# Moving the first MLP weight's products behind the last segment, with a reordered opening and refitted order tables

## The chip, the cores and the metric

One core of a Trainium2 chip. The time is device microseconds (us) of one execution; lower is better. A kernel counts as faster or slower from 2% on.

## The reference, cut to what matters

A recurrent attention over 64 segments of 32 tokens, with 8 memory tokens that come out of the segment before, and then an MLP over all 2048 tokens:

```python
for s in range(n_seg):                        # 64, one after the other: mem is carried
    h = concat([mem, x[s]])                   # 8 + 32 tokens, width 512
    q, k, v = h @ Wq, h @ Wk, h @ Wv          # 32 heads of 128
    p = softmax(where(mask, q @ k.T * scale, -1e9))
    o = (p @ v) @ Wo
    mem = o[:8]; outs.append(o[8:])
h = x + attention(layernorm(x))
out = h + gelu(layernorm(h) @ w1 + b1) @ w2 + b2      # F = 1792
```

Because of `mem` the segments can't overlap freely. What doesn't depend on the memory (the "B" products of a later block of four segments, here called filler work of the loop) is put between.

## The kernel before: the parts that matter

Segments are counted 0 to 63; four of them make a block of 128 tokens, so segments 4, 8, 12 ... are the first of a block. The kernel records operations and a list scheduler puts each on its engine by assumed times and by fitted priorities (`BONUS`). TensorE's order is given by a table, with a bank for each part:

```python
PHASE = (164, 250, 155, 235)
BONUS = {..., "nma": -1.85, ..., "xr": 5.47}                   # cut
ORDER = (("Q1", 0, 2), ("Q0", 0, 4), ("Q1", 2, 4), ("K0", 0, 4), ("K1", 0, 4), ("V0", 0, 4), ("SC0", 0, 99), ("F", 0, 1), ("SA", 0, 99), ("SC1", 0, 99),
         ("V1", 0, 4), ("F", 1, 2), ("PV0", 0, 99), ("F", 2, 3), ("PV1", 0, 99), ("WO", 0, 8), ("PVA", 0, 99), ("F", 3, 4))
```

Q, K and V are projections (L744, L490), SC0 and SC1 the two scores of the memory rows (L889), SA the scores of the other tokens (L947), PV0 and PV1 their products with the values (L919, L923), WO the output product (L1009), PVA the value product of the other tokens (L977), F the filler.

TensorE's instructions are fetched in pages of 256. `PHASE` says at which place of a page, modulo 256, each of the four kinds of segment shall begin; repeated weight loads serve as padding:

```python
if PHASE and o.tag is not None and o.tag[0] != seg:
    seg = o.tag[0]
    owed = (PHASE[seg % 4] - at) % FETCH_N        # FETCH_N = 256
    if owed > FETCH_N - SLIP:
        owed = 0
```

In the last block the filler place is taken by `w1_first`, four products of the first MLP weight and a Gelu on ScalarE:

```python
if bk == NTB - 1 and sg < 3:
    w1_first(2 * sg + r, BANK["F%d" % r])      # segments 60, 61, 62: six of the fourteen groups
```

## Time and profile before

858.89 us (three runs, 858.42 to 859.45). One profile:

| stretch | us | what |
|---|---|---|
| to 57.15 | 57.15 | opening: weights are loaded, segment 0 |
| 57.15 to 90.47 | 33.32 | segments 1 to 3, no filler |
| 90.47 to 695.22 | 604.75 | segments 4 to 59 ("the loop") |
| 695.22 to 749.61 | 54.39 | segments 60 to 63, up to the last output product |
| 749.61 to 780.61 | 31.00 | rest of the first MLP weight, MLP block 0 |
| 780.61 to the end | 76.29 | MLP blocks 1 to 3 |

The stretch table of the kernel before; columns are start:end, length, then busy time of PE, PEld, DVE, ACT and POOL with instruction counts, TensorE's granted clock, DMA share, GB/s. Rows that the prediction shows are left out:

```profile
57.15:90.47 33.32, 27.79 (x824) 18.63 (x1205) 25.98 (x82) 21.72 (x67) 11.50 (x30) 1.00 0.18 28
90.47:695.22 604.75, 601.04 (x17024) 346.43 (x18636) 495.19 (x1511) 439.55 (x1345) 196.19 (x525) 1.00 0.12 29
780.61:856.90 76.29, 72.91 (x330) 32.03 (x336) 16.35 (x24) 28.87 (x42) 17.66 (x16) 1.00 0.21 58
```

In the loop TensorE's records leave 604.75 - 601.04 = 3.7 us idle in 56 segments. (The ends of its products are modelled, so a short wait behind a product can hide in its record.)

### The profile page before, as it was taken

The page shows a single profiled execution, that of the slowest core. Times are in us where ns is not written, and L with a number is a line of the kernel's source. Part 1 is how long each engine was busy: PE and PEld are TensorE (multiplying, and loading weights), DVE is VectorE, ACT ScalarE, POOL GpSimd, SP SyncE. Part 2 cuts the span into 40 slices and gives each one's busy share as a digit, 9 for nine tenths or more (in the row PEclk, how much of TensorE's full clock was granted, in tenths as well). Part 3 has the DMA queues.
Part 4 walks back from the last instruction along what each step waited for, and adds up shares of the span by engine and source line. Part 5 has one row for each costly group of instructions (what it writes and reads, how often), then busy time and mean ns, then how long its engine had stood idle before and what let it go on. Part 6 is the DMA issues. An engine that isn't in the chain of part 4 may idle for free.

```text
span 856.9 us, 47407 instructions
## 1 busy us (share of the span) xinstructions
PE 804.1 (94%) x20064; PEld 448.2 (52%) x22282; DVE 597.3 (70%) x1782; ACT 561.7 (66%) x1609; POOL 263.5 (31%) x686
## 2 busy tenths in 40 slices
PE   3588999999999999999999999999999997799998
PEld 1245555556555555555555555555555553454443
DVE  3257777888787888788878787878787865533211
ACT  2346777777777777777777776777777778842332
POOL 3024114242424242333333324232414241047200
PEclk9879999999999999999999999999999999999999
DMA  9971000111101010101010101010122120154300
GB/s 345 352 196 22 10 17 23 29 29 29 29 25 32 24 34 24 33 23 35 22 35 20 36 21 33 19 26 17 28 47 52 47 78 16 39 177 120 86 25 24
DMA packets 66615, 48.80 MB, mean 57 GB/s; under 512 B 29156, under 2 KB 62828, under 8 KB 66412
## 3 DMA queue, kind: packets, MB, share of 16 engines
q1 hardware_dynamic: 66080, 45.50, 18.5%
q8 instruction: 166, 2.72, 1.4%
q14 instruction: 37, 0.30, 0.1%
q10 hardware_dynamic: 332, 0.27, 0.1%
HBM read 31.34 MB, written 8.39 MB: 46 GB/s over the span
## 4 chain that ended last, share of the span: by engine, by line
PE 84%; DVE 5%; ACT 5%; DMA 4%; issue 1%; SPq 0%; POOL 0%; ACTq 0%; DVEq 0%; POOLq 0%
PE ps L744 38%; PE ps L1009 13%; PE ps L490 8%; PE quad L1362 5%; PE ps L1355 4%; PE quad L919 3%; PE ps L1036 3%; PE quad L977 2%; PE quad L889 2%; ACT EC L901 2%; PE ps L947 2%; DMA WQ<-in_A_Wq_dram 1%; DVE TT L1021 1%; PE ps L1164 1%; DVE hT L1015 1%
## 5 line engine op out<-in xcount | busy, mean ns | idle before, releaser
L762 ACT CAST OT<-quad 128x128 bf16<-128x128 f32 (+1 forms) x192 | 85.0, 442 | 119.1 <-PE quad L977 78.8
L970 POOL COPY BD<-PTA 32x192 bf16<-32x192 bf16 x256 | 87.5, 342 | 228.7 <-DVE PTA L966 216.8
L744 PE MATMUL ps<-WQ,hT 128*32 128x512 bf16 x2048 | 124.8, 382 | 9.8 <-DVE hT L1015 8.0
L1009 PE MATMUL ps<-WO,OT 128*32 128x256 bf16 x4224 | 130.7, 275 | 1.5 <-ACT OT L762 1.5
L744 PE MATMUL ps<-WV,hT 128*32 128x512 bf16 x1780 | 121.4, 380 | 0.5 <-issue 0.5
L1009 PEld LDWEIGHTS ps<-WO,OT 128*32 128x32 bf16 x4224 | 107.4, 97 | 10.6 <-issue 2.6
L763 ACT ACTIVATE kq<-ps 128x512 bf16<-128x512 f32 x146 | 80.4, 596 | 48.2 <-PE ps L744 47.7
L744 PE MATMUL ps<-WK,hT 128*32 128x512 bf16 x1544 | 107.9, 380 | 0.0
L742 PEld LDWEIGHTS <-hT 128*32 128x32 bf16 x3652 | 60.3, 96 | 63.7 <-DVE hT L1015 38.0
L762 ACT CAST kq<-ps 128x512 bf16<-128x512 f32 x146 | 86.1, 591 | 11.2 <-PE ps L744 6.0
L785 DVE STREAM_TRANSPOSE KALL<-kq 128x256 f32<-128x256 f32 x160 | 68.9, 437 | 27.8 <-ACT kq L762 24.8
L762 ACT CAST VS<-ps 128x512 bf16<-128x512 f32 x124 | 72.4, 584 | 16.4 <-PE ps L744 14.1
L901 ACT ACTIVATE EC<-quad,nmc 128x64 f32<-128x64 f32 x252 | 76.8, 310 | 9.1 <-DVE nmc L897 3.6
L744 PEld LDWEIGHTS ps<-WV,hT 128*32 128x32 bf16 x1780 | 48.1, 96 | 42.1 <-issue 19.3
L744 PEld LDWEIGHTS ps<-WK,hT 128*32 128x32 bf16 x1544 | 46.4, 96 | 43.4 <-issue 23.2
L785 DVE STREAM_TRANSPOSE QT<-kq 128x256 f32<-128x256 f32 x128 | 55.7, 436 | 14.7 <-ACT kq L763 10.6
L919 PEld LDWEIGHTS quad<-PTC,VS 32*128 32x128 bf16 x2048 | 24.5, 92 | 75.9 <-ACT OT L762 29.1
L744 PEld LDWEIGHTS ps<-WQ,hT 128*32 128x32 bf16 x2048 | 55.0, 94 | 17.3 <-issue 1.7
L1358 ACT ACTIVATE WQ<-ps,b1t 128x512 bf16<-128x512 f32 x42 | 28.9, 687 | 52.8 <-PE ps L1355 52.8
L806 POOL COPY ZC<-QTB 128x256 bf16<-128x256 bf16 x64 | 25.3, 398 | 118.6 <-PE quad L889 81.9
L960 DVE TENSOR_REDUCE sma<-SA 128x8 f32<-128x256 f32 x64 | 26.8, 419 | 43.4 <-ACT SA L959 43.4
L490 PE MATMUL ps<-WK,hT 128*32 128x512 bf16 x504 | 51.5, 379 | 0.0
(155 smaller groups left out, 1516.6 us busy)
## 6 DMA issues: line engine op xcount, KB each, us to landing
WV<-in_A_Wv_dram SPq DMA_DIRECT2D x4, 1024.0 KB, 10.2
WK<-in_A_Wk_dram SPq DMA_DIRECT2D x4, 1024.0 KB, 19.2
v_last<-VSB SPq DMA_DIRECT2D x64, 64.0 KB, 2.5
WQ<-in_A_Wq_dram SPq DMA_DIRECT2D x4, 1024.0 KB, 10.2
VBD<-v_last SPq DMA_DIRECT2D x64, 64.0 KB, 2.5
WO<-in_A_Wo_dram SPq DMA_DIRECT2D x16, 256.0 KB, 7.5
h_mid<-xr SPq DMA_DIRECT2D x16, 128.0 KB, 2.0
WQ<-h_mid SPq DMA_DIRECT2D x4, 512.0 KB, 4.3
```

The lines of the kernel that those rows point to most:

```text
L490: return e.add_instruction(mybir.InstMatmult(name="I-%d" % (4000000 + _kept[0]), engine=mybir.EngineType.PE, start_tensor_calc=start, stop ...
L742: e.ldweights(l, tile_position=(0, 32 * j))
L744: ins = e.matmul(o, l, m, start=(k == 0), stop=(k == DC - 1), tile_position=(0, 32 * j), skip_group_check=True)
L762: return {"act": (lambda e: e.copy(out, src), t_act(n, ps_)), "dve": (lambda e: e.tensor_copy(out, src), 0.16 + 1.042e-3 * n * fast)}
L763: return {"act": (lambda e: e.mul(out, src, scale_), t_act(n, ps_)), "dve": (lambda e: e.tensor_scalar(out, src, scale_, None, ALU.mult), ...
L785: S.op("dve", lambda e: e.transpose(out, src), reads=[("kq", i)], writes=[key], dur=t_dve(256) + 0.02)
L901: ins = e.activation(EC[:, r, sl, :], o[:, sl, :], ACTF.Exp, bias=nmc[:, r, sl:sl + 1], accum_out=smc[:, r, sl:sl + 1])
L919: e.matmul(quad[:, j, (4 * r + i) * 16:(4 * r + i) * 16 + 16], VS[rows, s % 3, r, i * E:(i + 1) * E], PTC[rows, r, c0:c0 + 16, i // 2], st ...
L970: S.narrow(S.op("pool", lambda e, j=j, rows=rows: e.tensor_copy(BD[rows, par, :, j, :, :], PTA[rows, :, 0:NA, :]), reads=["PTA"], writes=[ ...
L1009: ins = e.matmul(ps[bank][32 * j:32 * j + 32, 0:256], lhs(slot(h)), wo_cols(h, b), start=(k == 0), stop=(k == 15), tile_position=(0, 32 * ...
L1355: ins = e.matmul(ps[bank][:, 0:SBT], W1[:, cc, fc * P:(fc + 1) * P], hnT_of(k)[:, cc, :], start=(cc == 0), stop=(cc == DC - 1))
L1362: S.op("pe", lambda e: e.matmul(quad[:, t, :], gT_of(k, fc)[:, t * P:(t + 1) * P], W2[:, fc, :], start=(fc == 0), stop=(fc == FC - 1)), re ...
```

## The change

Intent: take the Gelus, and with them the activation table loads, out of the last segments; bring the weights in before the value fetch of block 0; drop the filler in the opening; and fit TensorE's order, the banks, the priorities and the page phases anew.

```diff
-PHASE = (164, 250, 155, 235)
+PHASE = (109, 215, 114, 200)
-BONUS = {...}                                    # ~75 fitted priorities, all new; cut
+BONUS = {...}
-ORDER = (("Q1", 0, 2), ("Q0", 0, 4), ("Q1", 2, 4), ("K0", 0, 4), ("K1", 0, 4), ("V0", 0, 4), ("SC0", 0, 99), ("F", 0, 1), ("SA", 0, 99), ("SC1", 0, 99), ("V1",
-         0, 4), ("F", 1, 2), ("PV0", 0, 99), ("F", 2, 3), ("PV1", 0, 99), ("WO", 0, 8), ("PVA", 0, 99), ("F", 3, 4))
+ORDER = (("Q0", 0, 4), ("K0", 0, 4), ("Q1", 0, 4), ("K1", 0, 4), ("SC0", 0, 99), ("V0", 0, 4), ("V1", 0, 2), ("SC1", 0, 99), ("SA", 0, 99), ("V1", 2, 4), ("F",
+         0, 2), ("PV0", 0, 99), ("F", 2, 3), ("PV1", 0, 99), ("WO", 0, 8), ("PVA", 0, 99), ("F", 3, 4))
-         ("B", "Q", 1, (1, 6)), ("T", "WO", 3, 5), ("W", 7, 4), ("T", "WO", 5, 6), ("W", 7, 4), ("T", "WO", 6, 7), ("W", 7, 4), ("T", "WO", 7, 8))
+         ("B", "Q", 1, (1, 6)), ("T", "WO", 3, 8))
-                if bk == NTB - 1 and sg < 3:
-                    w1_first(2 * sg + r, BANK["F%d" % r])
-                chain[10:10] = spread["in", 0]
+                chain[14:14] = spread["in", 0]
-        for fc in range(6, FC):
-            w1_first(fc, (4, 5)[fc % 2])
-            rest[fc - 6]()
+        for fc in range(FC):
+            w1_first(fc, early[fc % 2])
+            rest.get(fc, lambda: None)()
```

(Cut: the new banks, the list of loads in the last segments, the new places of the remaining output products in `rest`, and two lines that follow from the move.)

## The prediction

> **What bounds the kernel now.** I read the stretch table first, cut where TensorE starts segments 1, 4, 56 and 60, the last output product of segment 63, the second MLP product and the second MLP block.
>
> ```profile
> core 0: us, PE busy (x) PEld busy (x) DVE busy (x) ACT busy (x) POOL busy (x), PEclk, DMA share, GB/s
> 90.47:652.00 561.53, 558.25 (x15808) 321.63 (x17302) 460.20 (x1405) 408.50 (x1250) 182.74 (x489) 1.00 0.11 28
> 695.22:749.61 54.39, 42.52 (x1066) 23.41 (x1313) 31.39 (x101) 45.62 (x101) 12.76 (x34) 0.97 0.13 37
> 749.61:767.86 18.25, 16.38 (x289) 9.38 (x282) 8.58 (x23) 8.44 (x13) 7.83 (x20) 1.00 0.53 159
> 767.86:780.61 12.75, 11.98 (x55) 5.32 (x55) 1.30 (x3) 0.69 (x1) 6.56 (x18) 1.00 0.58 153
> ```
>
> Segments 4 to 55 take 561.53 / 52 = 10.80 us each, TensorE nearly always busy. The last four take 54.39 us up to the last output product; there TensorE is busy only 42.5 and ScalarE 45.6. The chain of waits there, for segment 61:
>
> ```profile
> 709.48 1.92 PE ps L744 x32
> 714.63 1.28 ACT L901
> 719.15 1.28 ACT L1168
> 720.45 0.69 ACT hT L1168
> 721.71 1.28 ACT L959
> 724.94 1.92 PE ps L744 x32
> ```
>
> Segment 61 lasts 724.94 - 709.48 = 15.46 us, and three 1.28 us pieces of its chain are activation table loads: a Gelu (L1168) stands between two Exps (L901, L959). Next the opening: the chain, then stretches of 2 us.
>
> ```profile
> 20.39 7.36 DMA v_last<-VSB
> 30.11 10.95 DMA WQ<-in_A_Wq_dram
> 54.83 0.97 PE ps L713 x4
> 56.18 0.46 DVE TT L1021
> 57.15 1.92 PE ps L744 x32
> ```
> ```profile
> 30.00:32.00 2.00, 2.00 (x34) 0.86 (x25) 0.45 (x1) 0.80 (x2) 0.00 (x0) 0.71 1.01 182
> 36.00:38.00 2.00, 0.24 (x8) 0.00 (x0) 0.89 (x2) 1.27 (x4) 0.00 (x0) 1.00 1.03 409
> 48.00:50.00 2.00, 1.89 (x80) 1.71 (x84) 1.22 (x3) 1.16 (x5) 0.00 (x0) 0.50 1.11 349
> 54.00:56.00 2.00, 2.00 (x23) 0.55 (x20) 0.00 (x0) 0.00 (x0) 0.00 (x0) 1.00 0.37 105
> ```
>
> The value store of block 0 lands at about 27.8; its fetch waits for that in the queue, and half of WQ stands behind the fetch. The queue runs thin (182 GB/s), WQ lands at 41.1, and TensorE idles from 36 to 41. Then it runs at half clock until 51.6. By 54 DMA is falling off, the output weights are in, and TensorE does filler (L713) between output products.
>
> **What the Trainium skill says.** "ScalarE: Activation LUTs", section "What ACT_TABLE_LOAD costs": a load is about 1283 ns, with some 1380 ns of drain. The trace agrees on 1.28; no drain shows (714.63 + 1.28 = 715.91, the Exp starts at 715.93), so I count 1.28 alone. The same page, "Table sets: the hidden batching unit", says to finish all calls of one set before switching; the change does that. "TensorE: Matmul & The Clock Gate", section "What's actually happening": the array falls to half clock after an idle window of about 3.4 us and recovers after as much sustained work. Here: five thin microseconds, then 0.50. Its "Architectural detail" section calls the queues of ScalarE and VectorE strict FIFO; so an early instruction of theirs that waits holds all later ones.
>
> **The change, part by part.**
>
> *Segments 60 to 63.* The instruction listing of the built program has 14 table loads before and 2 after. What is segment 61 without loads and Gelus? Subtracting three loads, 15.46 - 3.85 = 11.6, and the Gelus it no longer carries (two of 0.69, partly on the path) bring 10.2 to 11.6. The second way is segment 3, which has neither filler nor Gelu: 79.86 to 90.47, 10.61 us. The third is the chain in the new order, from durations of an ordinary segment: Q0, K0, Q1, K1 end at 4 x 0.865 = 3.46; first score to its reduce 0.39; but the new VectorE order puts the second score's reduce and the wide one (L957) ahead of the first probabilities, so the second score at 4.9 gives reduce 5.29, wide one 5.58, PC 5.97, transpose 6.31, first PV 6.69 with 0.15 hop; PV1 0.79 later, output product 0.24 later, and 2.95 from there to the next Q (508.19 to 511.14): 10.67. I take 10.65. The output product of segment 63 starts 7.7 into it. So 3 x 10.65 + 7.7 = 39.7, against 54.39: **-14.5**, with 0.2 kept for slips.
>
> *Work moved behind.* Six of 14 groups of the first MLP weight (four 512-column products at 0.2155, 0.86 us) now come after segment 63: 6 x 0.86 = 5.2. In the listing, up to four groups follow each other with no other product between, on two banks; Gelu 0.69 plus a hop of 0.25 against 0.86 costs about 0.1 at each of some five such places: +0.5. Against that, the old code waited 1.68 us for VectorE's TTB (752.5 to 754.2, the bank of the last block product); the new code picks two other banks: -1.7. Smaller gaps of the old stage (18.25 - 16.38 less that) mostly close, -0.5, while the one remaining table load and the first Gelu are hidden by an output product between groups 0 and 1. 18.25 + 5.2 + 0.5 - 1.7 - 0.5 = 21.7: **+3.5**. The transposes for MLP block 1, 0.72 us late before, now stand ahead of the last three pieces of the first weight, and have 3 us more: **-0.7**.
>
> *The opening.* In the new queue all of WQ and two pieces of WO go before the value fetch. Up to 30 us 10.87 MB have moved (282, 401 and 404 GB/s over ten each); WV, WK, WQ, first inputs and the value store are 13.1 MB; at 0.40 MB/us the rest takes 5.6: WQ is there at 35.6, when TensorE first asks (36.1). Its products then end at about 37.9 instead of 43.5. After that WO sets the pace: 17.56 MB with the fetch, the last 4.4 at 0.35 MB/us: 48.3, and 12 filler products (2.6 us) are gone. Output product 0.35, then 1.4 to segment 1: near 50 at best against 57.15. But TensorE, waiting for WO piece by piece, may be cold, which would cost about 2 in segment 1. I take **-5**.
>
> *The 56 ordinary segments.* Start to start on TensorE (segment from 500.26): six projections 5.19, scores and SA 0.48, PV 0.68, WO 1.87, PVA 0.45, filler 1.72, sum 10.39; the best segments take 10.68 because of three waits: first PV for its probabilities (0.16), second PV for the copy of the first (0.12), Q for memory (0.2). The new order brings score 0 forward by 1.3 us, which takes away only the first. Minus 0.16 if nothing new comes. But with score 0 at 3.46, K0 and its query copy have to be transposed by then, and VectorE has opT 0.53, PA 0.44, mask 0.25, PTA 0.31 and two block transposes (0.38 each) ahead; adding spacings I get 3.5 to 3.8. And L957 ahead of the probabilities pushes first PV to 6.7, nearly where it is (464 - 457.25 = 6.71). So a computed 10.65 to 10.76, against a best of 10.68 and a mean of 10.80. The 0.12 between mean and best are hiccups, which the refitted phases may change either way. I take -0.05 each: **-2.8**, give or take 4.
>
> Sum: -14.5 + 3.5 - 0.7 - 5 - 2.8 = -19.5; 858.9 - 19.5 = **839.4 us**.
>
> **Rivals.** (a) *The refit loses in the loop.* If score 0 waits 0.3 us for VectorE in most segments, 56 x 0.2 = +11 over my term: about 853. For it: VectorE is busy 460 of 561 us and strictly in order; the block's mask, transposes and opT are ahead of K0. Against it: back-to-back transposes start 0.33 to 0.40 apart, less than their 0.45, and somebody refitted all priorities. (b) *The refit wins in the loop*, 0.15 a segment, hiccups included: -8 instead of -3, about 834. For it: 0.48 us of waits stand in each best segment. Against it: the wait for memory and the one between PVs are untouched. (c) *The opening gains little*, as WO is transfer-bound and TensorE stays cold without the filler: -2, total 842. The 0.50 clock for ten microseconds after only five thin ones speaks for it; that WQ no longer leaves that hole, against. (d) *The tail takes back more*: the normalisation of MLP block 1 (L1113, four of about 0.36) stands on VectorE before PTA of segment 63 and waits for its load; if that lands later than about 7 us after the output product, PVA of segment 63 and all Gelus behind its copy wait: +2 to 3.
>
> **Range and chances.** The table-load term is good to 1.5, tail 1.5, opening 2.5, loop 4; independent, that is about 5.2, so 80% is some 6.7 either side: 832.5 to 846.5. The 2% line lies near 841.9, just above the centre: faster 0.66, same 0.33, slower 0.01.
>
> **What will show it.** Table loads: two; segments 60 to 62 at 10.4 to 10.9 between first Q products. Output product of segment 63 to the second MLP product: 21 to 22.5. WQ landed before 37, no half clock at 42 to 46, segment 1 from 51 to 53. Mean of segments 4 to 55 at 10.68 to 10.82; if above 10.85 with TensorE waiting for KALL or ZC at the first score, rival (a) is right; below 10.68, rival (b). The prediction falls if the last segments stay over 11.5 (then the loads were not the cause), or if the loop moves by over 0.15 a segment.

## More of the kernel before

The residual addition of a finished block waits for a DMA transpose, and stands on VectorE, a strict queue, where the scheduler thinks the transpose will be done (its assumed time is worked out from the 256):

```python
def nat(bk):
    S.dma(lambda e: e.dma_start_transpose(oN[:], opT[:, bk % 2]...), 256, reads=[...], writes=["oN"])       # L1055, cut
    S.op("dve", lambda e: e.tensor_tensor(xs, xs, oN[:]..., ALU.add), reads=["oN", ("xr", bk % XR)], ...)   # L1058, cut
```

## The result, and the profile after

850.37 us (four runs, 849.34 to 852.85) against 858.96 us for the kernel before beside it. The ratio is 0.9904, 95% interval 0.9882 to 0.9927: within 2%, and 11 us above the predicted time, outside the predicted range of 832.5 to 846.5. All outputs are right. (Ratios are the mean time of one kernel's runs over that of the other's of the same rounds, so not quite the ratio of the medians.)

The stretch table of the changed kernel, cut at the same events. The profiled run is the slowest of the four (852.85 us), so the differences below sum to -5.9 us, those of the medians to -8.6:

```profile
54.16:89.36 35.20, 30.17 (x825) 21.46 (x1186) 24.95 (x82) 22.17 (x67) 11.39 (x30) 0.92 0.18 33
89.36:698.67 609.31, 601.79 (x17025) 334.69 (x18637) 467.21 (x1554) 443.05 (x1303) 195.78 (x526) 1.00 0.11 29
698.67:740.03 41.36, 36.05 (x1041) 22.11 (x1344) 29.55 (x95) 28.97 (x89) 12.65 (x34) 0.96 0.12 34
740.03:761.82 21.79, 21.78 (x313) 11.26 (x306) 8.54 (x22) 12.64 (x19) 12.18 (x32) 1.00 0.77 205
761.82:773.90 12.08, 12.08 (x57) 5.49 (x56) 3.28 (x6) 0.71 (x2) 6.58 (x10) 1.00 0.31 92
773.90:851.00 77.10, 73.23 (x337) 32.04 (x335) 14.38 (x22) 28.88 (x42) 13.46 (x12) 1.00 0.20 55
```

| stretch | before | after | difference | predicted |
|---|---|---|---|---|
| opening | 57.15 | 54.16 | -3.0 | -5, with segments 1 to 3 |
| segments 1 to 3 | 33.32 | 35.20 | +1.9 | |
| loop, segments 4 to 59 | 604.75 | 609.31 | +4.6 | -2.8 |
| segments 60 to 63 | 54.39 | 41.36 | -13.0 | -14.5 |
| to the second MLP product | 18.25 | 21.79 | +3.5 | +3.5 |
| MLP block 0 | 12.75 | 12.08 | -0.7 | -0.7 |
| rest | 76.29 | 77.10 | +0.8 | 0 |

The loop is where the sign was wrong. TensorE's busy time in it is the same within a microsecond (601.0 and 601.8); its idle time doubled, from 3.7 to 7.5 us. The idle time lies in two kinds of place. The first, in TensorE's timeline of segment 12 (start, length, engine, line, operands, count, idle before):

```profile
182.57 0.39 PE L490 MATMUL ps<-WK,hB 128*32 128x512 bf16 x4
182.90 0.23 PE L919 MATMUL quad<-PTC,VS 32*128 32x16 bf16 x9
183.99 0.21 PE L919 MATMUL quad<-PTC,VS 32*128 32x16 bf16 x7 [0.86 <-issue]
184.17 0.40 PE L1009 MATMUL ps<-WO,OT 128*32 128x256 bf16 x8
```

and of segment 28, the same products without the gap:

```profile
357.39 0.39 PE L490 MATMUL ps<-WK,hB 128*32 128x512 bf16 x4
357.72 0.40 PE L919 MATMUL quad<-PTC,VS 32*128 32x16 bf16 x16
357.96 0.21 PE L923 MATMUL quad<-PTC,VBD 32*128 32x64 bf16 x4
```

The second PV stops after its ninth product, for a reason that the profile can't name ("issue"). By the listing of the built program a page border lies there: instruction 18 of the 40 of PV1. The border before it is at the end of score 0 (31 of 32). The Trainium skill, "Runtime: NRT & Kernel Launch", section "Instruction fetch mechanics", says that instructions come in pages of 16 KiB (256 instructions), fetched by DMA while the page before runs, at a cost it calls "mostly hidden". The page size agrees: the instruction queue of TensorE moved 2.72 MB in 166 packets, 16 KB each. The DMA view of 178.9 to 184.4 us, segment 12 from the end of score 0 on; its first line is the rate in 40 slices of 0.1375 us:

```profile
GB/s 0 60 0 0 0 0 0 0 0 0 0 0 0 0 0 0 0 119 0 0 0 0 0 0 0 0 0 0 0 0 0 0 0 0 0 0 0 0 0 0
q8 instruction: 1, 0.02, 1.5%
```

The one packet of that queue (q8) starts in the 18th slice, 2.28 us after score 0, and lands 1.28 later; nothing else is on the DMA engines at that moment. PV1 goes on 1.5 us after the landing. In segment 28 the packet starts 0.93 after score 0, and nothing stops. This holds in all seven profiles with a border in that part of PV1 (segments 8, 12 ... 56, 91 in all; the runs are told below): in 33 the packet started 2.1 to 2.8 us after score 0, and all 33 stalled, by 0.21 to 0.89 us; in 58 it started 0.4 to 1.5 us after, and none of them lost more than 0.07 us there. In all 33, PV1 went on 1.2 to 1.6 us after the packet had landed; in the other 58 it had landed at least 1.7 us before the first product behind the border. (`old_prio`, told below, has the border too, but far longer segments, and is not counted; there the seven that stalled by 0.5 us or more are again those with a late packet.) In the changed kernel these stalls come to 3.2 us in five first segments, and two stops of PVA, also "issue", to 1.1 more.

The second kind of place, on VectorE in the second segment of a block (segment 29):

```profile
364.06 0.18 DVE L799 COPY ZC<-QT 128x128 bf16<-128x128 bf16 x1
364.95 0.42 DVE L1058 TENSOR_TENSOR xr<-xr,oN 128x512 bf16<-128x512 bf16 x1 [0.70 <-DMA oN<-opT]
365.29 0.44 DVE L785 STREAM_TRANSPOSE QT<-kq 128x256 f32<-128x256 f32 x1
365.65 0.25 DVE L897 TENSOR_REDUCE nmc<-quad 128x2 f32<-128x128 f32 x1
365.83 0.42 DVE L785 STREAM_TRANSPOSE KALL<-kq 128x256 f32<-128x256 f32 x1
```

```profile
366.40 0.28 PE L889 MATMUL quad<-KALL,ZC 128*32 128x64 bf16 x13 [0.23 <-DVE KALL L785]
```

The residual addition L1058 waits 0.70 us for its transpose, and all VectorE work of the second score stands behind it; 1.5 us later TensorE waits for its keys. Five second segments have such a wait of TensorE, 1.6 us in all. The list of waits (total, times, longest), before and after:

```profile
DVE xr L1058 <- DMA oN<-opT: 11.2, 2, 10.2
```
```profile
DVE xr L1058 <- DMA oN<-opT: 13.3, 9, 5.1
```

Two waits in the MLP at the end are all of the first total and 8.8 us of the second. In the loop there were none before; now there are seven, 4.5 us in all.

A measure for both: in every profile but one told below, the shortest segments of the loop, from one output product to the next, last 10.68 or 10.69 us. What a segment takes above 10.68, summed over the 14 segments of each kind, I call its excess. Before: 4.1 in first, 1.4 in second, 1.2 in third and fourth segments of the blocks. After: 6.8, 3.3 and 1.1.

### The profile page after: what moved, and what is told of

The parts are those of the page before. It is cut to its first block, busy times and chain, and to the rows that moved or that the text cites. A ratio compares the mean times of both kernels' runs of the same rounds, so it can differ in the third digit from the quotient of the medians.

```text
span 851.0 us, 47411 instructions
## 1 busy us (share of the span) xinstructions
PE 801.9 (94%) x20061; PEld 438.9 (52%) x22307; DVE 566.5 (67%) x1818; ACT 553.2 (65%) x1561; POOL 265.3 (31%) x686
## 3 DMA queue, kind: packets, MB, share of 16 engines
q8 instruction: 166, 2.72, 1.3%
## 4 chain that ended last, share of the span: by engine, by line
PE 84%; DMA 5%; DVE 3%; POOL 3%; SPq 2%; issue 2%; ACT 1%; ACTq 0%; POOLq 0%; DVEq 0%
PE ps L744 36%; PE ps L1009 13%; PE ps L490 10%; PE quad L1357 6%; PE ps L1350 4%; PE ps L1036 4%; PE quad L919 3%; PE quad L977 3%; DMA oN<-opT 2%; PE quad L889 2%; PE ps L947 2%; PE ps L1164 2%; POOL opT L1050 2%; SPq L671 1%; DMA xr<-in_A_x_dram 1%
## 5 line engine op out<-in xcount | busy, mean ns | idle before, releaser
L744 PE MATMUL ps<-WV,hT 128*32 128x512 bf16 x1780 | 132.7, 381 | 0.0
L762 ACT CAST kq<-ps 128x512 bf16<-128x512 f32 x160 | 92.5, 588 | 34.0 <-PE ps L744 32.1
L763 ACT ACTIVATE kq<-ps 128x512 bf16<-128x512 f32 x160 | 92.6, 600 | 21.1 <-PE ps L744 20.8
L742 PEld LDWEIGHTS <-hT 128*32 128x32 bf16 x3942 | 65.8, 98 | 59.3 <-DVE hT L1015 30.8
L762 ACT CAST VS<-ps 128x512 bf16<-128x512 f32 x127 | 74.4, 586 | 0.0
L744 PEld LDWEIGHTS ps<-WV,hT 128*32 128x32 bf16 x1780 | 41.7, 95 | 33.4 <-issue 21.0
L744 PEld LDWEIGHTS ps<-WQ,hT 128*32 128x32 bf16 x1796 | 48.1, 95 | 19.8 <-issue 8.8
```

Source lines behind the costliest of these rows:

```text
L742: e.ldweights(l, tile_position=(0, 32 * j))
L744: ins = e.matmul(o, l, m, start=(k == 0), stop=(k == DC - 1), tile_position=(0, 32 * j), skip_group_check=True)
L762: return {"act": (lambda e: e.copy(out, src), t_act(n, ps_)), "dve": (lambda e: e.tensor_copy(out, src), 0.16 + 1.042e-3 * n * fast)}
L763: return {"act": (lambda e: e.mul(out, src, scale_), t_act(n, ps_)), "dve": (lambda e: e.tensor_scalar(out, src, scale_, None, ALU.mult), ...
```

## The experiments

Theory: the tail and the opening did what they should, within some microseconds; the refit lost in the loop, by pages fetched late and by the waiting addition. Rivals: the loss has nothing to do with the refit; the new part order itself is worse; the profile was an unlucky one.

| run | median us | ratio to before | loop | excess first / second |
|---|---|---|---|---|
| (before) | 858.96 | 1 | 604.75 | 4.1 / 1.4 |
| (after) | 850.37 | 0.9904 | 609.31 | 6.8 / 3.3 |
| tail_only | 845.64 | 0.9856 | 604.73 | 4.5 / 1.6 |
| refit_only | 864.25 | 1.0075 | 612.28 | 10.5 / 2.3 |
| no_refit | 843.63 | 0.9833 | 603.91 | 3.5 / 0.9 |
| nma_late | 851.59 | 0.9922 | 607.87 | 3.3 / 5.2 |
| phase114 | 850.41 | 0.9922 | 608.66 | 6.1 / 3.7 |
| on_later | 850.86 | 0.9918 | 609.51 | 9.5 / 0.6 |
| warm_back | 851.50 | 0.9917 | 610.00 | 8.3 / 2.9 |
| page50 | 848.06 | 0.9864 | 608.46 | 2.0 / 7.4 |
| page50_on | 842.95 | 0.9804 | 604.33 | 2.4 / 1.4 |
| page50_on_warm | 842.39 | 0.9798 | 605.36 | 2.2 / 2.7 |
| no_refit_warm | 845.91 | 0.9837 | 604.76 | 3.5 / 1.6 |
| after_again | 852.67 | 0.9924 | 609.60 | 7.2 / 2.9 |
| no_refit_again | 843.32 | 0.9814 | 604.24 | 3.2 / 1.8 |
| page50_on_again | 843.13 | 0.9811 | 603.27 | 1.7 / 1.5 |
| page60_on | 844.73 | 0.9835 | 604.83 | 2.5 / 1.8 |

(Loop and excess are from one profile each, in us. The sets ran on different chips; each ratio is to the kernel before on the same chip, whose median was 857.96 to 860.16, so across sets the ratios are safer than the medians. `old_prio`, 945.14 us, is told below.)

**First set: which part of the change does what.**

`tail_only`: the kernel before, with the moved products alone.

```diff
 PHASE, BONUS, ORDER, START as before
-                    w1_first(2 * sg + r, BANK["F%d" % r])
+        for fc in range(FC): w1_first(...)        # all behind segment 63
```

> The kernel before with only the last part of the change: all sixteen groups of the first MLP weight behind segment 63; old opening, old part order, priorities and phases. My theory of the result (the tail gives what I predicted, about -14.5 + 3.5 - 0.7, and the refitted loop is what lost): segments 60 to 63 some 13 to 15 us shorter, the loop as before (604.7 us for 56 segments), total 846 to 849 us. Rival (the refit belongs to the tail change and the old order does badly without the moved products): the last segments stay over 11.2 us each, total above 851.

(The groups are fourteen, not sixteen.) Measured 845.64 us, ratio 0.9856 (0.9841 to 0.9871). Three rows of its stretch table answer to the prediction's three terms of the tail:

```profile
693.68:733.73 40.05, 35.16 (x1043) 22.01 (x1344) 30.17 (x95) 28.54 (x89) 12.54 (x34) 1.00 0.16 44
733.73:755.40 21.67, 21.66 (x311) 11.32 (x305) 8.77 (x23) 12.53 (x19) 12.28 (x31) 1.00 0.65 171
755.40:767.49 12.09, 12.09 (x57) 5.47 (x56) 3.28 (x6) 0.72 (x2) 6.18 (x9) 1.00 0.48 130
```

-14.3, +3.4 and -0.7 against the kernel before, for -14.5, +3.5 and -0.7. It alone is faster than the whole change.

`refit_only`: the kernel before with the new `ORDER`, `BANK`, `BONUS` and `PHASE` alone.

> The kernel before with only the refitted tables: part order, banks, priorities and phases; old opening, old place of the first MLP weight's products. My theory (the refit costs about 4.6 us in the ordinary segments, by TensorE stalls inside the second PV and by the waits of VectorE's residual addition for its transpose): total 861 to 865 us, loop near 609 us for the 56 segments. Rival (the loss in the loop comes from somewhere else, for instance from the opening's order shifting the transfers): total 857 to 860, loop near 605.

Measured 864.25 us, 0.75% slower than before (1.0045 to 1.0105), with the loop at 612.28. The refit is what loses.

`no_refit`: the whole change with those four tables as before.

> The whole change without the refitted tables: new opening and moved products, but the part order, banks, priorities and phases of before. My theory: the loop is back at about 605 us for the 56 segments, opening some 1 to 3 us shorter than before, total 844 to 848 us, faster than the changed kernel by 3 to 6. Rival (the refit is neutral, the excess in the loop follows from opening or chance): total within 1.5 us of the changed kernel, 849 to 852.

Measured 843.63 us, 0.9833. The refit cost 850.37 - 843.63 = 6.7 us here, and 0.0075 x 858 = 6.4 without the rest of the change: within the noise it adds up, so the refit did not need the moved products to do harm, nor they it. The opening alone is tail_only to no_refit: -2.0. (After_again and no_refit_again, on one chip in the fourth set, differ by 9.4 us, 5.4 of them in the loop: the refit's cost is known to some 3 us only.)

`nma_late`: the changed kernel with one priority put back, so that the wide maximum L957 stands behind both probabilities on VectorE.

```diff
-"nma": 7.54
+"nma": -1.85
```

> The changed kernel with one priority of its table put back to the old value, that of the wide negated maximum (7.54 to -1.85): on VectorE the first and second probabilities and their transposes then stand ahead of it instead of behind. My theory (the earlier first score bought nothing because the wide maximum stood before the first probabilities; without it first PV comes about 0.12 us earlier per segment): best segments 10.55 to 10.60 instead of 10.68, total 842 to 846 us. Rival (the segment is bound by other waits, the first PV's wait just moves to the next): best segments 10.66 to 10.70, total 849 to 852.

Measured 851.59 us, best segments 10.68: my theory fell, and the rival held. The earlier probabilities did nothing for the best segments. The excess moved from first to second segments (3.3 and 5.2); its sum over both fell from 10.1 to 8.5 and the loop by 1.4 us, but not the total.

**Second set: one suspected cause at a time.**

`phase114`: the borders in first segments five instructions earlier.

```diff
-PHASE = (109, 215, 114, 200)
+PHASE = (114, 215, 114, 200)
```

> The changed kernel with one number different: the place in TensorE's instruction stream at which the first segment of a block starts is 114 instead of 109 modulo 256, so that the borders between instruction pages lie after score product 26 of 32 and after 13 of 40 in the second PV, as they do in the third segment of a block, which shows no stall. My theory (the gaps of 0.65 and 1.03 us inside the second PV of the first segments, and their other excess, are instruction fetches that come late): mean period of these segments falls from 11.2 to 10.8 us, 57th minus 4th segment shorter by 3 to 6, total 845 to 848 us. Rival (the fetch is late wherever the border falls, because of the queue or of what else the DMA engines carry): the gaps move or stay, total 849 to 853.

Measured 850.41 us: the rival's number. The stalls moved with the border, from behind the ninth product of PV1 to behind the sixth, in four segments instead of five. A border inside PV1 is bad at either place.

`on_later`: the residual addition nine instructions later on VectorE, by a longer assumed time of its transpose.

```diff
-            S.dma(lambda e: e.dma_start_transpose(oN[:], ...), 256,
+            S.dma(lambda e: e.dma_start_transpose(oN[:], ...), 1000,
```

> The changed kernel with the assumed time of the transpose that feeds VectorE's residual addition raised by some 2 us, which moves that addition nine instructions later in VectorE's order, behind both probabilities; TensorE's order is the same. My theory (the addition waits for its transpose in front of the score's work, 4.0 us in total, and TensorE's second segments of a block pay for it): those segments fall from 10.95 to 10.75 on average, total 846.5 to 848.5 us. Rival (TensorE had slack there, or the addition now holds up the shared head's softmax): total 849 to 852.

The second segments fell as expected, from 3.3 to 0.6 of excess, but the first ones rose from 6.8 to 9.5, seven of them stalling at the page border instead of five, and the total stayed: 850.86 us. Its waits:

```profile
DVE xr L1058 <- DMA oN<-opT: 5.9, 1, 5.9
```

`warm_back`: the twelve filler products of the old opening put back.

```diff
-         ("B", "Q", 1, (1, 6)), ("T", "WO", 3, 8))
+         ("B", "Q", 1, (1, 6)), ("T", "WO", 3, 5), ("W", 7, 4), ("T", "WO", 5, 6), ("W", 7, 4), ("T", "WO", 6, 7), ("W", 7, 4), ("T", "WO", 7, 8))
```

> The changed kernel with the twelve filler products put back between the last pieces of the output weights in the opening, nothing else. My theory (without them the clock is at half speed through segment 1): first to fourth segment 33.2 to 33.8 us instead of 35.2, segment 1 starting within 0.5 of 54.2, total 848 to 849.5 us. Rival (the clock falls anyway, because of the waits for the weights): stretch 34.8 to 35.4, total within 1 us of the changed kernel or up to 1 above it.

Stretches of 4 us of the changed kernel, then of this run, same columns as above (the clock is third from the end):

```profile
50.00:54.00 4.00, 1.37 (x20) 0.35 (x17) 0.93 (x4) 0.00 (x0) 0.00 (x0) 0.50 0.76 236
54.00:58.00 4.00, 3.85 (x37) 2.76 (x114) 2.39 (x6) 0.72 (x2) 1.58 (x4) 0.50 0.46 125
```
```profile
50.00:54.00 4.00, 3.14 (x32) 1.07 (x32) 0.65 (x3) 0.00 (x0) 0.42 (x2) 1.00 0.77 236
54.00:58.00 4.00, 3.63 (x61) 2.61 (x174) 3.56 (x11) 2.08 (x4) 1.58 (x4) 1.00 0.26 74
```

The filler keeps the clock at full speed, and segments 1 to 3 take 33.32 instead of 35.20, as expected. The total did not follow (851.50): the loop of this profile is 0.7 longer. The stretch is shown, the gain is not.

`old_prio`: the changed kernel with the old priorities.

```diff
-BONUS = {... new ...}
+BONUS = {... as before ...}
```

> The changed kernel with the priorities of before, but the new part order, banks and phases. This divides the refit, which cost 6.7 us in all. Theory one (the new part order itself is at fault, with score 0 right behind the keys and two scores inside the value products): total stays 849 to 853 us. Theory two (the order is sound, the fitted priorities are at fault): total 843 to 846 us. If the priorities only fit their own order: above 854, and then the two can't be told apart this way.

Measured 945.14 us, 12.3 us per segment in the loop: the third case. Priorities fit one order only, and this run can't tell which of the two is at fault. It is the exception to the 10.68.

**Third set: both causes.**

`page50`: all four phases 50 larger. VectorE's and ScalarE's listings are the same, TensorE's differ in repeated weight loads alone, and SyncE's in the place of a few transfers near the end. Borders now lie in a key projection, the first PV, SA and WO, much as in the old order.

```diff
-PHASE = (109, 215, 114, 200)
+PHASE = (159, 9, 164, 250)
```

> The changed kernel with all four of its phases 50 larger: the same instructions in the same order on every engine (only repeated weight loads on TensorE as padding differ), but the borders of TensorE's instruction pages lie in a key projection, the first PV, the shared scores and the output product, as in the old order, instead of in score 0, the second PV and the shared PV. Theory (the late issues are a fetch that comes too late for the short products behind the border): the excess of the first segments of the blocks over 10.68 us falls from 6.8 (summed over 14) to 3 to 4, total 845.5 to 848 us. Rival (a page border costs the same wherever it lies, or something else holds up TensorE there): excess 6 to 9, total 849 to 852.

Measured 848.06 us. The excess of the first segments fell from 6.8 to 2.0, below what I had expected. But that of the second ones rose from 3.3 to 7.4: the waits of the addition,

```profile
DVE xr L1058 <- DMA oN<-opT: 17.9, 14, 5.3
```

now come 14 times, 12 of them in the loop. None of the "issue" stops is left in PV1 or PVA of its first segments. It fits that a first segment which doesn't stall gives the transpose less time; that was argued, not tried by itself. And MLP blocks 1 to 3 take 76.32 again instead of 77.1, in all kernels with moved borders: that +0.8 was the borders too.

`page50_on`: both at once.

```diff
 PHASE as in page50, assumed transpose as in on_later
```

> The run before with the residual addition moved later on VectorE as well. Theory (the two causes add up, and the later addition gave nothing alone only because the late fetches ate it): excess of first and second segments 3 to 4 and 0.6, loop 603.5 to 605 us, total 842.5 to 845.5. Rival (a gain in one kind of segment is lost in the other, as when the addition alone was moved: there is a third thing that holds the block to its time): loop 608 to 610, total 848 to 851.

842.95 us, 0.9804 (0.9791 to 0.9818, on both sides of the 2% line: unclear). Alone the borders gave 2.3 and the addition nothing; together they give 7.4 (by the ratios 3.4, nothing and 8.6). Each fault had hidden part of the other. And the new part order, which is kept here, is not what lost: the rival falls.

`page50_on_warm` and `no_refit_warm`: the filler of the opening added to page50_on and to no_refit.

> The same with the twelve filler products of the old opening put back. Theory (filler keeps the clock up in segments 1 to 3, worth about 1 to 1.9 us there, and nothing else changes): first to fourth segment 33.0 to 33.4 us, total 1 to 1.5 us below the run before. Rival (the loop gives it back, as when filler alone was put back): within 0.7 of the run before.

> The kernel with the moved products and the new opening order but the old part order, banks, priorities, phases (843.6 us before) and the old filler. If filler is worth what the cold clock costs in the opening of that kernel (33.57 against 33.05 us for segments 1 to 3): 842.8 to 843.5 us. Rival (filler delays the output products that it stands between): 843.7 to 844.5.

842.39 us (840.76 to 843.99), and segments 1 to 3 at 31.90, the shortest of all, but no more than 0.6 below page50_on, whose runs overlap with it: the rival. The other, 845.91, is above even the rival's range, but the chip differs from no_refit's: the ratios, 0.9837 and 0.9833, are the same, so the filler gained nothing there. In all three pairs the loop of the one profile with filler was longer than without, by 0.4 to 2.1 us. Why is open.

**Fourth set, side by side on one chip.** Does the loss repeat, and does mending the refit beat dropping it?

> The changed kernel itself once more, on the same chip as the three others of this set. If the loss in the ordinary segments belongs to the kernel and not to one execution: excess of the first segments of the blocks over 10.68 us again 6 to 11 in all, of the second ones 2.5 to 4, total 849 to 852 us. Rival (the first profile was an unlucky one): excess below 5 and 2, and a total that agrees with it, below 848.

852.67 us, excess 7.2 and 2.9: it repeats.

> The change without the refit once more, beside the mended version. Expected 843 to 845 us, and excess 3 to 4 and 1 in first and second segments. If it is at or below the mended version's time, then undoing the refit is as good as mending it, and the refit brought nothing at all.

> The mended version (page borders moved, residual addition later) once more, beside the one without the refit. Theory (the refit's order is worth some 0 to 3 us once its two faults are mended): 841.5 to 844 us, and 0.5 to 2.5 below the version without the refit. Rival (the earlier difference came from different chips): within 0.5 us of it or above.

843.32 and 843.13 us: 0.2 apart, the rival. Their loops, no_refit_again first:

```profile
88.28:692.51 604.23, 600.72 (x17024) 345.92 (x18635) 495.27 (x1512) 439.53 (x1345) 196.26 (x525) 1.00 0.12 29
```
```profile
87.76:691.02 603.26, 601.66 (x17024) 339.54 (x18636) 470.14 (x1554) 442.16 (x1303) 195.66 (x525) 1.00 0.12 29
```

TensorE is busy 99.4 and 99.7% of the loop. The mended refit leaves 1.6 us of idle time instead of 3.5, and needs 0.9 us more of busy time; 25 us less work on VectorE count for nothing.

`page60_on`: the borders ten instructions further, `PHASE = (169, 19, 174, 4)`.

> The mended version with phases 60 instead of 50 larger: the borders move ten instructions, from a key projection to a query projection and from 21 to 11 of 40 in the first PV; no border falls into score 0, the second PV or the shared PV. Theory (what counts is which products stand behind the border, not the exact place): within 2 us of the mended version. Rival (each place has its own cost): more than 3 us away.

844.73 us, 1.6 above page50_on_again: within the 2 us of the theory. In this one step, what stands behind the border mattered more than the exact instruction.

## Why the prediction was right or wrong, point by point

- **Segments 60 to 63, -14.5.** Right. Without the refit it is -14.3. In the changed kernel's profile it was -13.0 (-14.3 in after_again), because segment 60 lost some 1.9: its output product stopped after seven products, again with "issue" as the cause, and then the granted clock fell to half for 3.4 us (708.1 to 711.5). nma_late and on_later show such a fall in segments 60 to 63 too, each in a segment that lost 1.5 us or more; after_again and tail_only have none.

```profile
706.29 0.40 PE L1009 MATMUL ps<-WO,OT 128*32 128x256 bf16 x7
707.39 2.76 PE L1009 MATMUL ps<-WO,OT 128*32 128x256 bf16 x57 [0.70 <-issue]
```

- **Work moved behind, +3.5, and MLP block 0, -0.7.** Right: +3.5 (+3.4 without the refit) and -0.7. Two table loads are left, and TensorE is busy 21.78 of 21.79 us there.
- **The opening, -5.** The failing step is "the queue runs thin (182 GB/s)". The same row said DMA share 1.01: the engines were full, and moved little. Putting the value fetch behind the weights moved this stretch from 30-36 to 36-42 us and did not remove it. The DMA view of 36 to 42 us of the changed kernel and then of 32 to 36:

```profile
DMA packets 1812, 1.53 MB, mean 254 GB/s; under 512 B 139, under 2 KB 1792, under 8 KB 1811
q1 hardware_dynamic: 1811, 1.51, 112.0%
```
```profile
DMA packets 595, 1.59 MB, mean 398 GB/s; under 512 B 35, under 2 KB 263, under 8 KB 595
q1 hardware_dynamic: 595, 1.59, 102.7%
```

  At a full share, packets of 0.84 KB on average moved 254 GB/s and packets of 2.7 KB 398. The Trainium skill, "DMA: Bandwidth & Descriptors", section "Why small descriptors are slow (HBM only)", names a fixed cost per packet; the direction agrees, but size is not all: in the kernel before, from 30 to 36 us, packets of 1.85 KB on average moved no more, 252. Packet by packet, the value fetch's are 512 B and took 45 to 49 ns, and while they ran the weights' packets were slower too: 4 KB in 240 ns (before, 30 to 36 us) and 1 KB in 69 (after, 36 to 42), instead of 164 and 49 (after, 32 to 36). So the last quarter of WQ landed at 38.8, not 35.6, and the last piece of WO at 52.2, not 48.3, as the chain of the changed kernel has it:

```profile
45.41 6.78 DMA WO<-in_A_Wo_dram
52.19 0.14 issue
52.32 0.64 PE ps L1009 x7
```

  The second part, the cold clock ("would cost about 2"), was inside the -5 as a possibility and came true: +1.9. Over all profiles (three with the old opening, eleven with the new one without filler; old_prio left out) segment 1 starts 2.3 earlier, at 53.9 against 56.2, and segments 1 to 3 take 1.2 longer, 34.3 against 33.05. So -1.1, where -5 was taken; rival (c), with -2, was nearest.
- **The loop, -2.8.** This is the term that decided; it came out at +4.6. Of the 11 us that the total was off, some 7 are here and some 4 in the opening. Two steps failed. The first is "the best segments take 10.68 because of three waits", of which the new order would take away the first, 0.16. The sum didn't close: 10.39 and waits of 0.48 are 10.87, not 10.68. The end of the first probabilities (L908) and the first PV in a best segment before (segment 46), then in the changed kernel (segment 26), other lines left out:

```profile
550.08 0.24 DVE L908 STREAM_TRANSPOSE PTC<-PC 128x64 f32<-128x64 f32 x1
550.09 0.40 PE L490 MATMUL ps<-WV,hB 128*32 128x512 bf16 x4
550.48 0.27 PE L919 MATMUL quad<-PTC,VS 32*128 32x16 bf16 x16
```
```profile
335.00 0.25 DVE L908 STREAM_TRANSPOSE PTC<-PC 128x64 f32<-128x64 f32 x1
335.13 0.41 PE L490 MATMUL ps<-WV,hB 128*32 128x512 bf16 x4
335.47 0.26 PE L919 MATMUL quad<-PTC,VS 32*128 32x16 bf16 x16
```

  Before, the first PV starts 0.36 us after the last product ahead of it and 0.15 after its probabilities; in the changed kernel 0.31, with the probabilities 0.23 old; in nma_late again 0.31, with them 0.5 us old or more (medians of the best segments). So there was a wait, but of 0.05, not 0.16, and the rest of the new order took nearly all of it back, half of it in the scores and SA (0.48 to 0.51 us): the best segments last 10.69 and 10.68. The second PV stands 0.31 behind its predecessor in all three, its probabilities 0.15 to 0.39 old: no wait for them shows. The wait for memory before Q (0.40) is the same in all. From start to start, projections and filler take 7.4 us where I had 5.19 + 1.72 = 6.91, and the two PVs 0.48 where I had 0.68; that is the 0.3 that the sum of 10.39 was short. The second step that failed is "hiccups, which the refitted phases may change either way", put at nothing: they went from 6.7 to 11.2 us. Both their causes are shown: page50 and on_later each take one away, page50_on both, and then the loop is at 603.3 to 604.3.
- **Rival (a)** named the sign (+11 by a wait of score 0 for VectorE) with the wrong mechanism for most of it. Score 0 is late by some 0.05 us in most first segments; the time goes to the pages and to the addition. Rivals (b) and (d) did not come: the loop grew, and the work behind segment 63 took the +3.5 of the prediction.
- **What was not foreseen:** +0.8 in the last MLP blocks, by the page borders, and the half clock in segment 60.

With both faults mended the change gives 842.95 us, 3.6 above the prediction and inside its range, though not by the loop's gain: its loop is 0.4 to 1.5 us below the old one, where -2.8 was taken. What starts the page fetch at 0.9 us after score 0 in one segment and at 2.3 in the next stays open: no other packet is in its way, TensorE's waits around it are the same in both, and nma_late had one late fetch in 13.

## What to carry to other kernels

Before hoping for a gain from a new order, take the busy time of the bounding engine in the stretch from its length: the idle time is about what an order could win here (3.7 of 605 us; TensorE's busy time in the loop stayed between 600.7 and 603.6 us in all runs but old_prio). A wait that hides in a modelled record shows in the steps from start to start: it is one only if the step shrinks when the operand comes earlier. A refit of an order has to be scored on the chip with the instruction stream that it makes, since a page border inside a run of short products can cost as much as the whole gain. Where two hiccups follow each other in a recurrence, mend both before judging either.

## What the Trainium skill lacked or had wrong

- "Runtime: NRT & Kernel Launch", "Instruction fetch mechanics", calls the cost of a page border mostly hidden. Here a border inside a run of short TensorE products cost 0.21 to 0.89 us in 33 of 91 passes, always when the fetch had started over 2 us after the border before, and at most 0.07 us otherwise. The page has no figure for how long a page takes to arrive: the packet took 0.9 to 1.4 us, and where it was late, execution went on 1.2 to 1.6 us after it had landed.
- "TensorE: Matmul & The Clock Gate", "What's actually happening", speaks of idle windows, without a figure for how little activity makes a window idle. Here TensorE was busy 1.51 of the 3.41 us before 49.3 us, with no wait over 1.1 us, and the clock fell to 0.50; in warm_back, busy 2.74 of the same 3.41 us, it kept 1.00.
- "ScalarE: Activation LUTs", "What ACT_TABLE_LOAD costs", adds a drain of some 1380 ns to a load. None shows here on either side: each of the twelve loads of segments 60 to 63 took 1.28 us, began 0.02 us after the copy before it had ended, and was followed 0.01 us later.
- "DMA: Bandwidth & Descriptors", "Why small descriptors are slow (HBM only)", has a cost of 3 cycles per packet beside one per 32 bytes. By that, 1 KB packets cost an estimated 7% more per byte than 4 KB ones; measured without the value fetch were 49 ns and 164, 20% more. With the fetch beside them the same sizes took 69 and 240 ns, which a cost per packet doesn't explain. No run here tells why; the scattered places that the fetch goes to are a guess.
